# A convolution beside a gated unit on one core: a weight load placed behind the first power, and a new order of work

## The chip, the cores and the metric

The kernel runs on one core of a Trainium2 chip. The core has five engines that run their own instruction streams and meet through semaphores: TensorE (PE in the profile: matmuls, with weight loads shown as PEld), VectorE (DVE), ScalarE (ACT), GpSimd (POOL) and SyncE (SP, which here only issues DMAs). ACT and POOL issue a few DMAs too. Times are device microseconds of one execution; the time of a kernel is the median of its runs.

## The reference, cut to what matters

```python
x = A_u                                    # 2048 tokens x 512 channels, bf16
xn = layernorm(x)
# part A: a state-space convolution along the tokens, per channel d
dt = exp(log_dt)[:, None]
P = exp((dt * (A_re + 1j*A_im))[:, :, None] * arange(2048))   # 512 x 128 modes x 2048 lags
K = einsum("dn,dnl,dn->dl", Cc, P, dt * Bc).real
yA = irfft(rfft(pad(xn^T)) * rfft(pad(K)))[..., :2048]^T + xn * Dskip
# part B: a gated linear unit, 512 -> 1792 -> 512
yB = (sigmoid(xn @ w_gate) * (xn @ w_up)) @ w_down
return x + yA + yB
```

## The kernel before

**Layer norm.** The tokens are 16 groups of 128. `layernorm` (from L530) computes a group's statistics either on DVE (L542 to L544) or, for the groups in `ON_ACT`, on ACT (three activations with accumulated sums, the last at L537). GpSimd raises the variances of a stretch of groups to the power -0.5 (L495), DVE makes the bias from it (L499), and DVE (L556) or ACT normalises. The first four groups are transposed on PE (L565) and copied to `xnT`; the other twelve are stored to `x_scr` in stretches of four and come back by transposing DMAs.

**Gated unit.** Four groups of 512 tokens by 14 blocks of 128 features. Per block there are four matmuls with `wg_sb` (L1031), a sigmoid on ACT (L1040), four matmuls with `wu_sb` (L1046) and a product on DVE (L1061). The product reads the up result either from PSUM or, for the block numbers in `UEV` (14 x group + block), from `us_sb`, to which ACT has copied it (L1057). Then, for every 128 tokens, 14 matmuls with `wd_sb` (L1090), whose result is evicted to `glu_sb`.

**Convolution.** First `f_n` (L665, L667 on DVE, the squares at L656 on ACT) squares a complex number per channel and mode eleven times; GpSimd issues two DMAs per step (`f_cw`, L661) that convert the f32 result to bf16 tables `W`. Then, for four chunks of 128 channels, DVE builds two tables, G (16 entries) and H (41 entries), by complex products: `f_a` (L722, L723) multiplies, `f_b` (L727, L728) adds; some entries of H are squares made by ACT (L775) and DVE (L780, L781), and some are seeds copied from `W`. PE multiplies them in two halves (`f_k`, L806), selects (L827, L831), and the result becomes `kT`. The tokens go through small transforms: `fx` (L684, with the constant S1 and the normalised tokens), a store to `z_scr` and a load, then, for 8 pairs of units, four to each of two halves of the channels, `fm` (L874, with `m2`), `fk` (L890, with constants streamed from `c_E`), elementwise products on DVE (L895, L899), sums of them (`fsum`, L906, L907, L909), and the transform back, on PE. `SUMS` says for each pair how much is summed first: 0 means nothing and 64 matmuls (`fv`, L923), 1 means L906 and L907 and 32 matmuls (`fvs`, L935), 2 means L909 as well and 16 matmuls. The result is stored to `v_scr`, loaded again and finished by `fy` and with the last down blocks.

**The order.** The function describes 981 operations in the order of the code through `_Plan.add`: an engine, an estimated cost, a function that emits the instructions, and the operations that it depends on. `add` notes these dependencies in `users` and `left`, for a planner that isn't in the file. With `ORDER` written out, `run` goes through that list, binds the buffers and yields the operations; each engine gets its instructions in that order:

```python
        for n in ORDER or range(len(self.ops)):
            op = self.ops[n]
            for s in op.acq:
                s.idx = self.free[s.pool].pop(0)
```

The semaphores between engines come from the framework, which follows what each instruction reads and writes. `_Plan.copy` (L291 on DVE, L293 on ACT) emits a copy on DVE if its operation's number is in `ON_DVE` and on ACT otherwise.

**Loads.** `load` (L427 is the line that every DMA of this helper shows) adds a DMA on a queue. `l_wd` is the load of all down weights, 1792 KB in one DMA on SP's queue; it is operation 16. The first readers of `wd_sb` are the down matmuls of the first 128 tokens.

## Time and profile before

| | us |
|---|---|
| runs | 215.34, 214.74, 214.60 |
| median | 214.74 |
| profiled execution | 214.40 |
| its span, from the first to the last instruction | 212.7 |
| the load of the down weights, issue to landing | 15.8 |
| PE, first gate matmul | 9.18 |

The granted TensorE clock of the profiled execution is 0.998. The page cuts the span into 40 slices of 5.3 us and prints the busy share of each in tenths; these are its rows for four engines and for the DMA engines.

```profile
PE   7999998999998999999999999999999999999993
DVE  3999999998999999999999999999999999876773
ACT  3899999999999999898999999979499999632000
POOL 3324033138121000000000003700010000004000
DMA  6999939934889406798266377661997986989924
```

A row shows where an engine is full and not what it waits for: PE and DVE are at 9 nearly from end to end, DVE thins out over the last six slices, and ACT does so a little earlier. In other views a row is "start, duration, engine, line, operation, output<-inputs, sizes, count", and brackets at its end give the idle time before it and the instruction that ended it. [...]

### The profile page before, as it was taken

The page shows a single profiled execution, that of the slowest core. Times are in us where ns is not written, and L with a number is a line of the kernel's source. Part 1 is how long each engine was busy: PE and PEld are TensorE (multiplying, and loading weights), DVE is VectorE, ACT ScalarE, POOL GpSimd, SP SyncE. Part 2 cuts the span into 40 slices and gives each one's busy share as a digit, 9 for nine tenths or more (in the row PEclk, how much of TensorE's full clock was granted, in tenths as well). Part 3 has the DMA queues.
Part 4 walks back from the last instruction along what each step waited for, and adds up shares of the span by engine and source line. Part 5 has one row for each costly group of instructions (what it writes and reads, how often), then busy time and mean ns, then how long its engine had stood idle before and what let it go on. Part 6 is the DMA issues. An engine that isn't in the chain of part 4 may idle for free.

```text
span 212.7 us, 5745 instructions
## 1 busy us (share of the span) xinstructions
PE 205.2 (96%) x2251; PEld 103.2 (49%) x2251; DVE 196.2 (92%) x423; ACT 174.8 (82%) x359; POOL 33.0 (16%) x66
## 2 busy tenths in 40 slices
PE   7999998999998999999999999999999999999993
PEld 2564443444443454445466466544555646444452
DVE  3999999998999999999999999999999999876773
ACT  3899999999999999898999999979499999632000
POOL 3324033138121000000000003700010000004000
PEclk9999999999999999999999999999999999999999
DMA  6999939934889406798266377661997986989924
GB/s 188 369 420 362 278 97 232 180 54 109 175 202 228 128 5 197 215 230 253 79 182 204 99 237 207 107 101 35 277 290 201 308 252 174 296 226 244 275 102 148
DMA packets 44045, 42.36 MB, mean 199 GB/s; under 512 B 8810, under 2 KB 37747, under 8 KB 44019
## 3 DMA queue, kind: packets, MB, share of 16 engines
q1 hardware_dynamic: 39074, 36.95, 56.8%
q0 software_dynamic: 4512, 4.73, 14.1%
q8 instruction: 17, 0.28, 0.6%
q10 hardware_dynamic: 432, 0.33, 0.5%
q14 instruction: 10, 0.07, 0.1%
HBM read 25.21 MB, written 12.07 MB: 175 GB/s over the span
## 4 chain that ended last, share of the span: by engine, by line
PE 55%; DVE 30%; ACT 7%; issue 2%; POOL 2%; DMA 1%; DVEq 0%; ACTq 0%; POOLq 0%
PE bank L1090 15%; PE bank L1031 11%; PE bank L1046 10%; PE bank L890 8%; DVE hT_sb L1061 5%; ACT big L293 4%; DVE big L667 3%; DVE big L665 3%; DVE stats L542 3%; DVE big L723 2%; DVE big L722 2%; PE bank L923 2%; PE bank L806 2%; PE bank L874 2%; DVE big L604 2%
## 5 line engine op out<-in xcount | busy, mean ns | idle before, releaser
L293 ACT ACTIVATE big<-bank 128x512 bf16<-128x512 f32 (+2 forms) x147 | 77.6, 652 | 5.0 <-PE bank L806 2.9
L1031 PE MATMUL bank<-xnT,wg_sb 128*128 128x512 bf16 (+1 forms) x244 | 54.1, 362 | 1.1 <-DVE hT_sb L1061 0.7
L1046 PE MATMUL bank<-xnT,wu_sb 128*128 128x512 bf16 x224 | 52.8, 379 | 0.1
L1090 PE MATMUL bank<-wd_sb,hT_sb 128*128 128x512 bf16 (+1 forms) x238 | 50.9, 367 | 0.3 <-ACT glu_sb L293 0.2
L1040 ACT ACTIVATE hT_sb<-bank 128x512 bf16<-128x512 f32 x56 | 33.3, 648 | 3.4 <-PE bank L1031 3.4
L1090 PEld LDWEIGHTS <-hT_sb 128*128 128x128 bf16 x238 | 22.5, 98 | 25.9 <-issue 2.3
L1031 PEld LDWEIGHTS <-wg_sb 128*128 128x128 bf16 x244 | 22.7, 98 | 25.2 <-issue 4.9
L1046 PEld LDWEIGHTS <-wu_sb 128*128 128x128 bf16 x224 | 21.4, 98 | 26.3 <-issue 2.1
L722 DVE TENSOR_TENSOR big<-big 128x1024 bf16<-128x1024 bf16 (+4 forms) x40 | 27.2, 679 | 0.0
L723 DVE TENSOR_TENSOR big<-big 128x1024 bf16<-128x1024 bf16 (+4 forms) x40 | 27.0, 676 | 0.0
L895 DVE TENSOR_TENSOR big<-big 128x2048 bf16<-128x2048 bf16 x16 | 19.5, 1225 | 0.6 <-ACT big L293 0.4
L1057 ACT ACTIVATE us_sb<-bank 128x512 bf16<-128x512 f32 x29 | 19.2, 665 | 0.7 <-DVE hT_sb L1061 0.7
L890 PE MATMUL bank<-big 128*128 128x256 bf16 x160 | 19.6, 273 | 0.0
L1061 DVE TENSOR_TENSOR hT_sb<-hT_sb,bank 128x512 bf16<-128x512 bf16 x27 | 17.7, 684 | 0.4 <-ACT hT_sb L1040 0.4
L890 PEld LDWEIGHTS <-big 128*128 128x128 bf16 x160 | 15.4, 98 | 4.9 <-issue 1.0
L727 DVE TENSOR_TENSOR big<-big 128x512 bf16<-128x512 bf16 (+4 forms) x40 | 17.0, 425 | 0.0
L728 DVE TENSOR_TENSOR big<-big 128x512 bf16<-128x512 bf16 (+4 forms) x40 | 17.0, 424 | 0.0
L661 POOL DMA_DIRECT2D big<-big x24 | 13.0, 546 | 24.6 <-DVE big L667 23.4
L775 ACT ACTIVATE sq_sb<-big 128x256 bf16<-128x256 bf16 (+2 forms) x20 | 14.3, 715 | 2.0 <-DVE big L728 2.0
L293 ACT ACTIVATE big<-big 128x256 bf16<-128x256 bf16 x31 | 14.5, 480 | 0.4 <-PE bank L806 0.4
L1061 DVE TENSOR_TENSOR hT_sb<-hT_sb,us_sb 128x512 bf16<-128x512 bf16 x29 | 12.0, 424 | 0.0
L656 ACT ACTIVATE big<-big 128x1024 f32<-128x1024 f32 x11 | 11.9, 1079 | 0.0
(99 smaller groups left out, 213.5 us busy)
## 6 DMA issues: line engine op xcount, KB each, us to landing
big<-c_E SPq DMA_DIRECT2D x16, 320.0 KB, 4.7
z_scr<-big SPq DMA_DIRECT2D x16, 256.0 KB, 2.8
big<-z_scr SPq DMA_DIRECT2D x16, 256.0 KB, 4.6
v_scr<-big SPq DMA_DIRECT2D x16, 256.0 KB, 3.0
big<-big POOLq DMA_DIRECT2D x24, 128.0 KB, 3.6
big<-in_A_u_dram SPq DMA_DIRECT2D x4, 512.0 KB, 9.0
big<-v_scr SPq DMA_DIRECT2D x4, 512.0 KB, 4.4
wu_sb<-in_B_w_up_dram SPq DMA_DIRECT2D x2, 896.0 KB, 13.2
```

What stands on the lines that cost most here:

```text
L293: nc.scalar.activation(out=get(out), in_=get(in_), func=ACT.Identity)
L722: V.tensor_tensor(out=wide(outp), in0=wide(lo), in1=mre, op=ALU.mult)
L723: V.tensor_tensor(out=wide(tb()), in0=wide(lo), in1=mim, op=ALU.mult)
L727: V.tensor_tensor(out=outp[:, :, 0], in0=outp[:, :, 0], in1=tb()[:, :, 1], op=opr)
L890: T.matmul(bank(sk[kt == NKT - 1])[:, DW * c:DW * c + DW], es()[:, c, kt, :], kT[p][:, kt, :], start=kt in (0, NKT - 1), stop=kt >= NKT - 2)
L895: V.tensor_tensor(out=pp()[:, :, 0:4, :], in0=xx()[:, :, 0, :].unsqueeze(2).to_broadcast([128, 2, 4, DW]), in1=kb().unsqueeze(1).to_broadc ...
L1031: T.matmul(bank(sl)[:, c0:c1], w_at(w, CUT_G, kt, k), xnT[:, grp, kt, c0:c1], start=(kt == 0), stop=(kt == KT - 1))
L1040: S.activation(out=hT_sb[:, hs.idx, k % 2, :], in_=bank(sl), func=ACT.Sigmoid)
L1046: T.matmul(bank(sl), w_at(wu_sb, CUT_U, kt, k), xnT[:, grp, kt, :], start=(kt == 0), stop=(kt == KT - 1))
L1057: S.activation(out=us_sb[:, us.idx, :], in_=bank(sl), func=ACT.Identity)
L1061: V.tensor_tensor(out=h(), in0=h(), in1=us_sb[:, us.idx, :] if on else bank(sl), op=ALU.mult)
L1090: T.matmul(bank(po)[:, 0:c[1] - c[0]], hT_sb[:, hts[k // 2].idx, k % 2, jj * 128:(jj + 1) * 128], wd_sb[:, k, c[0]:c[1]], start=first and ...
```

## The change

The call that loads the down weights is moved from among the other loads to behind the description of the powers, and gets a dependency, `deps=[W_op[0]]`, on the first conversion. It becomes operation 87; operations 17 to 87 become 16 to 86, and the others keep their numbers. Five lists are replaced: `SUMS` (one pair of the second half of the channels goes from 2 to 1), `UEV` (29 entries become 34), `ON_DVE` (19 become 22), `ON_ACT` (token group 15 leaves it) and the whole of `ORDER`. Nothing else is changed.

```diff
 UNITS = ((0, 1, 2, 3, 4, 5, 6, 7), (0, 1, 2, 3, 4, 5, 6, 7))
-SUMS = ((0, 0, 0, 1), (1, 2, 1, 1))
+SUMS = ((0, 0, 0, 1), (1, 1, 1, 1))
...
-UEV = (5, 9, 11, 15, 16, 18, 21, 22, 24, 25, 27, 28, 29, 30, 31, 32, 33, 34, 35, 36, 37, 38, 39, 42, 43, 44, 45, 49, 54,)
+UEV = (3, 6, 8, 9, 10, 14, 15, 16, 18, 19, 20, 21, 24, 27, 28, 29, 30, 32, 33, 34, 35, 36, 37, 38, 39, 40, 41, 43, 44, 45, 46, 47, 51, 54,)
-ON_DVE = (95, 96, 97, 109, 118, 191, 193, 196, 230, 243, 375, 485, 488, 494, 507, 551, 587, 598, 600,)
+ON_DVE = (32, 95, 96, 97, 109, 118, 181, 192, 230, 289, 292, 328, 369, 489, 494, 504, 508, 517, 550, 578, 598, 601,)
-ON_ACT = (2, 8, 9, 10, 11, 13, 15,)
+ON_ACT = (2, 8, 9, 10, 11, 13,)
 ORDER = [
-    23, 0, 1, 24, 22, 29, 30, 19, 25, 2, 35, 3, 6, 10, 5, 31, 34, 43, 26, 27, 32, 36, 44, 7, 20, 37, 40, 28, 33, 21, 45,
-    38, 46, 47, 41, 39, 48, 42, 632, 626, 620, 621, 49, 633, 627, 622, 638, 634, 639, 90, 88, 89, 91, 644, 645, 655, 650,
-    4, 11, 628, 685, 92, 51, 50, 54, 656, 646, 675, 9, 55, 640, 676, 686, 93, 680, 52, 56, 53, 95, 15, 57, 58, 12, 13,
-    660, 661, 641, 665, 642, 94, 8, 635, 16, 670, 629, 647, 648, 666, 651, 681, 623, 690, 59, 60, 96, 636, 114, 637, 657,
...
+    0, 18, 23, 24, 2, 20, 1, 34, 3, 25, 26, 6, 10, 5, 22, 19, 14, 33, 28, 21, 42, 35, 29, 36, 39, 7, 40, 30, 31, 43, 37,
+    27, 41, 4, 32, 44, 45, 46, 11, 90, 91, 89, 50, 9, 15, 38, 626, 632, 47, 48, 13, 633, 620, 627, 621, 49, 12, 644, 638,
+    639, 645, 650, 655, 622, 646, 634, 665, 88, 53, 51, 651, 666, 656, 640, 685, 686, 55, 56, 628, 54, 670, 660, 671, 690,
+    623, 657, 641, 635, 92, 52, 691, 636, 101, 114, 57, 115, 58, 624, 625, 93, 629, 630, 631, 637, 87, 8, 647, 675, 672,
...
     load_x(8, 4)
     l_dk = load("SP", dskr[0:1, :], A_Dskip.rearrange("(o d) -> o d", o=1), 1 * KB)
     load_x(12, 4)
-    l_wd = load("SP", wd_sb[:], B_w_down.rearrange("(k p) d -> p k d", k=FT), 1792 * KB)
     l_m2 = load("SP", m2[:], cten["M2"].ap(), 256 * KB, pkt=2048)
     l_sw = load("SP", sw[:], cten["SW"].ap(), 96 * KB, pkt=768)
 
...
             cur_op = pl.add("DVE", 1.2, f_n, [s_op] + W_op[-2:-1], PLAD + k * 0.01)
         W_op.append(c_op)
 
+    l_wd = load("SP", wd_sb[:], B_w_down.rearrange("(k p) d -> p k d", k=FT), 1792 * KB, deps=[W_op[0]])
     layernorm(4, 8, PLN1)
     layernorm(8, 12, PLN2)
     layernorm(12, 16, PLN3)
```

## The prediction

> **What bounds the kernel now.** First the head of the page, then busy time in four stretches that I cut at the places where VectorE (DVE) hands work to TensorE (PE).

> ```profile
> span 212.7 us, 5745 instructions
> PE 205.2 (96%) x2251; PEld 103.2 (49%) x2251; DVE 196.2 (92%) x423; ACT 174.8 (82%) x359; POOL 33.0 (16%) x66
> ```
> ```profile
> core 0: us, PE busy (x) PEld busy (x) DVE busy (x) ACT busy (x) POOL busy (x), PEclk, DMA share, GB/s
> 3.58:76.69 73.11, 70.82 (x382) 32.37 (x381) 71.09 (x167) 70.08 (x138) 20.76 (x32) 1.00 0.79 213
> 76.69:150.97 74.28, 73.81 (x1160) 39.26 (x1160) 74.13 (x169) 68.94 (x151) 6.82 (x16) 1.00 0.60 162
> 150.97:184.92 33.95, 33.91 (x530) 18.97 (x528) 33.05 (x54) 31.25 (x64) 0.86 (x1) 1.00 0.87 256
> 184.92:212.70 27.78, 24.45 (x178) 11.75 (x176) 17.89 (x38) 3.28 (x7) 2.51 (x3) 0.99 0.72 201
> ```

> PE's 96% alone would say that PE is the bound. The stretches say more: from 3.58 to 150.97 DVE idles 2.02 + 0.15 us of 147.39, PE 2.29 + 0.47. Two engines are full at once, and DVE's results pace PE's convolution work. These are the first and last hand-overs, in the order of time on both engines, and PE's end.

> ```profile
> 76.25 0.44 DVE L728 TENSOR_TENSOR big<-big 128x512 bf16<-128x512 bf16 x1
> 76.49 1.67 PE L806 MATMUL bank<-big 128*32 128x82 bf16 x128 [0.18 <-ACT big L293]
> ...
> 183.90 0.55 DVE L906 TENSOR_TENSOR big<-big 128x768 bf16<-128x768 bf16 x1
> 184.37 0.55 DVE L907 TENSOR_TENSOR big<-big 128x768 bf16<-128x768 bf16 x1
> 185.13 0.86 PE L935 MATMUL bank<-big 32*64 32x512 bf16 x32
> ...
> 206.17 3.23 PE L1090 MATMUL bank<-wd_sb,hT_sb 128*128 128x256 bf16 x28
> ```

> L728 is the last step of chunk 0's table G; L806 (`f_k`) multiplies it and starts 0.24 after L728 does, having waited 0.18. At the end, L935 starts 0.2 after the last half-sum L907. From 76.49 on PE is full: the last matmul ends at 206.17 + 3.23 = 209.40, 132.91 us after `f_k` began. The profiled execution took 214.4, so 5.0 us lie behind that end. So the time is: when can `f_k` of chunk 0 start, plus PE's work from there.

> **The dependency that the change names.** `deps` fills a list that only the planner reads; with an order written out, the kernel emits in that order, and an engine waits only where two instructions touch the same tile. `wd_sb` shares no tile with the powers. I cost the named wait at nothing: it is not in the program. What is real is the place on SP's queue.

> ```profile
> 13.81 0.46 SPq L427 DMA_DIRECT2D wd_sb<-in_B_w_down_dram  x1
> ...
> wd_sb<-in_B_w_down_dram SPq DMA_DIRECT2D x1, 1792.0 KB, 15.8
> ...
> 34.15 0.40 PE L684 MATMUL bank<-big 32*64 32x512 bf16 x2
> ...
> 35.51 1.69 PE L1090 MATMUL bank<-wd_sb,hT_sb 128*128 128x512 bf16 x7
> ```

> The load is the fourteenth issue of SP in both orders. It lands at 13.81 + 15.8 = 29.6, 5.9 us ahead of its first reader (35.51). Moved past it are the load of S1 (32 KB, now behind it, first read at 34.15) and that of `dskr` (1 KB, now ahead); the load of tokens 8 to 11 goes ahead of the second half of the up weights. S1 keeps some 20 us from its issue to its reader, and the bytes in flight are the same. Cost nothing; the cover is the 5.9 us for the weights.

> **The order, DVE ahead of `f_k`.** I counted, engine by engine, what stands ahead of chunk 0's `f_k` in the two orders. DVE's queue ahead of it grows. Spacings, start to start, of the rows:

> ```profile
> 27.01 1.28 DVE L1061 TENSOR_TENSOR hT_sb<-hT_sb,bank 128x512 bf16<-128x512 bf16 x2
> 28.20 0.69 DVE L542 BATCH_NORM_STATS2 stats<-big 128x6 f32<-128x512 bf16 x1
> ...
> 29.21 1.27 DVE L1061 TENSOR_TENSOR hT_sb<-hT_sb,bank 128x512 bf16<-128x512 bf16 x2
> ...
> 35.37 0.27 DVE L291 COPY big<-big 128x256 bf16<-128x256 bf16 x1
> 35.50 0.68 DVE L1061 TENSOR_TENSOR hT_sb<-hT_sb,bank 128x512 bf16<-128x512 bf16 x1
> ...
> 76.60 0.42 DVE L1061 TENSOR_TENSOR hT_sb<-hT_sb,us_sb 128x512 bf16<-128x512 bf16 x1
> 76.93 1.22 DVE L722 TENSOR_TENSOR big<-big 128x2048 bf16<-128x2048 bf16 x1
> 78.07 1.22 DVE L723 TENSOR_TENSOR big<-big 128x2048 bf16<-128x2048 bf16 x1
> ```

> - Operation 237, two 128x2048 products of chunk 1, moves from just behind chunk 0's `f_b` to ahead of it: 2 x (78.07 - 76.93) = +2.28.
> - Token group 15's statistics go from ACT to DVE: 29.21 - 28.20 = +1.01.
> - The copy of the second transposed token tile goes to DVE (bf16, PSUM, 128x512). No row shows it there: above the 0.13 of a 128x256 copy from SBUF (35.50 - 35.37), below the 0.60 of a product that reads PSUM ((28.20 - 27.01)/2). I take 0.45, nearer the row with PSUM. Chunk 0's first G copy also goes to DVE, +0.13; two seed copies leave or fall behind, -0.27.
> - Products of the GLU (L1061): one that reads SBUF takes 76.93 - 76.60 = 0.33, from PSUM 0.60. Numbers 16 and 22 move ahead (+0.66), 19, 24 and 25 behind (-1.26). Of those ahead, seven go from PSUM to SBUF and four the other way: -3 x 0.26 = -0.79.

> Sum: 2.28 + 1.01 + 0.45 + 0.13 - 0.27 + 0.66 - 1.26 - 0.79 = **+2.21 us** on DVE. What comes off is a wait:

> ```profile
> 44.23 1.05 POOL L661 DMA_DIRECT2D big<-big  x2 [3.20 <-DVE big L667]
> 46.98 3.21 POOL L495 TENSOR_TENSOR ln_ri<-ln_ve,half 128x4 f32<-128x4 f32 x1 [1.70 <-ACT ln_ve L537]
> ...
> 50.22 0.16 DVE L499 SCALAR_TENSOR_TENSOR ln_nb<-mv,ln_ri 128x4 f32<-128x4 f32 x1 [0.92 <-POOL ln_ri L495]
> ```

> DVE stood 0.92 for the power -0.5 of tokens 8 to 11, which GpSimd began late because ACT's statistics were late. In the new order ACT makes these statistics at least 5 us sooner, ahead of copies that now follow. GpSimd then begins right behind its conversions, which follow a squaring step that stands about 1.5 us sooner: 44.23 + 1.05 - 1.5 = 43.8, ending near 47.0, while DVE, with more ahead of it, comes to L499 near 51.0. The 0.92 goes whole. `f_k` thus starts at 76.49 + 2.21 - 0.92 = **77.78**.

> **PE, ahead of `f_k` and behind it.**

> ```profile
> 11.08 8.46 PE L1031 MATMUL bank<-xnT,wg_sb 128*128 128x256 bf16 x52 [0.43 <-ACT xnT L293]
> ...
> 35.05 0.41 PE L684 MATMUL bank<-big 32*64 32x512 bf16 x6 [0.50 <-ACT us_sb L1057]
> ...
> 67.47 1.02 PE L1031 MATMUL bank<-xnT,wg_sb 128*128 128x512 bf16 x4 [0.71 <-DVE hT_sb L1061]
> ...
> 88.73 0.59 PE L1090 MATMUL bank<-wd_sb,hT_sb 128*128 128x512 bf16 x2 [0.18 <-ACT glu_sb L293]
> ...
> 123.39 0.95 PE L923 MATMUL bank<-big 32*64 32x512 bf16 x29 [0.21 <-DVE big L899]
> ```
> ```profile
> 164.12 0.97 PE bank L1031 x4
> ...
> 173.68 0.86 PE bank L1031 x4
> 174.54 0.57 PE bank L935 x16
> ...
> 179.99 0.79 PE bank L935 x32
> ```

> The second fence is from the chain of waits: start, time, matmuls. Ahead of `f_k` PE now has one up block more (0.86) and starts about 0.17 later by a hand count of the first loads. If none of its waits of 0.18, 0.43, 0.50 and 0.71 went, it would reach `f_k` at 76.49 + 0.86 + 0.17 = 77.5; if all went, at 75.7. DVE's 77.78 is later either way, so it sets the start.

> From `f_k` on: 132.91 - 0.86 (that up block) + 0.22 (`SUMS`: one pair's product sums are left to PE, 32 matmuls at 0.79 for 16 at 0.57) + 0.22 (two more changes of matmul layout, 0.97 - 0.86 = 0.11 each) - 0.39 (the waits of 0.18 and 0.21, which DVE's and ACT's earlier work removes) = 132.10. PE ends at 77.78 + 132.10 = 209.88, the execution at 214.88: 0.48 above its own 214.4. The runs' median is 214.74, so **215.2**.

> That later hand-overs don't become late is the weak step. DVE's whole work changes by +1.01 (statistics) + about 1.05 (fourteen copies in, eleven out, 0.35 each) - 1.30 (five more products read SBUF) - 0.94 (two sums fewer, 184.37 - 183.90 each): -0.2. DVE is no more loaded; the moved 2.28 is missing behind `f_k`.

> [...] GpSimd's power took 3.21 at 46.98, and there is a row of 1.39 for the same form:

> ```profile
> 14.83 1.39 POOL L495 TENSOR_TENSOR ln_ri<-ln_ve,half 128x4 f32<-128x4 f32 x1 [7.25 <-DVE ln_ve L544]
> ```

> [...]

> **The rivals.**
> - **A, as summed** (0.41): 215.2, between 214.6 and 215.8.
> - **B, faster** (0.25): the new order also closes DVE's small gaps ahead of `f_k` (2.02 - 0.92 = 1.10) and the unknown copy costs its lower bound (0.32 less). `f_k` starts at 77.78 - 1.42 = 76.36, still behind PE's 75.7; PE ends at 208.46, the run at 213.5, median 213.8. For it: PE has little else that could hold it. Against: those gaps are many and small, and nothing in the order names them.
> - **C, slower** (0.31): DVE waits again for the power on GpSimd. It decides if GpSimd ends after about 51.0, 4 us later than I count; that needs ACT's statistics late again, or a power over 7.2 us long. Then the 0.92 stays: 216.1. The same price comes from any one DVE wait of that length ahead of `f_k`, since PE has no slack behind it.
> - **D, the wait is real** (0.03): the load is issued after the first conversion.

> ```profile
> 17.48 1.32 POOL L661 DMA_DIRECT2D big<-big  x2 [1.25 <-DVE ln_nb L499]
> ...
> big<-big POOLq DMA_DIRECT2D x24, 128.0 KB, 3.6
> ```

> It would be issued at 17.48 + 1.32 + 3.6 = 22.4 and land at 38.2, 2.7 after its reader's 35.51. At least 0.3 of this is hidden by PE's wait for `f_k`: 215.2 + 2.4 = 217.6.

> **How the numbers follow.** Likeliest is A: 215.2. The range 213.5 to 217.0 holds A, B and C with their unknown copy (0.13 to 0.60) and leaves out D and the far ends. About 0.3% (0.64 us) is what a measurement of this kernel tells from no change. B falls below it: faster 0.25. C and D lie above: 0.34, to which A's upper edge adds 0.02. A's rest, 0.39, is within.

> **What would show it.** The trace after should have: the weights' load issued near 14, as before, without a wait for GpSimd; operation 237's two 1.22 us products ahead of chunk 0's last L728; no wait at L499 for the power; `f_k` near 77.8 and released by DVE; then PE unbroken for 132.1. A start of `f_k` before 76.9 speaks for B, a DVE wait of about 0.9 ahead of it for C. The forecast is wrong in kind if PE stands for DVE behind chunk 1, where I took all hand-overs to fit.

## The result, and the profile after

| | before | after |
|---|---|---|
| runs, us | 215.34, 214.74, 214.60, 214.22 | 216.35, 217.05, 218.37, 217.13 |
| median, us | 214.67 | 217.09 |
| profiled execution, us | 214.40 | 216.35 |
| its span, us | 212.7 | 214.4 |

The ratio of the times is 1.0117, with a 95% interval of 1.0084 to 1.015: the kernel became slower by about 1.2%, 2.4 us. The forecast was 215.2, so it had the sign of its middle value right and a size of one fifth, and the time lies 0.09 above its range. The profiled executions differ by 1.95.

The page's first lines, and the same four stretches as before (the last one ends with the span, at 214.40). The columns of the second fence are stretch, length, busy time of PE, PEld, DVE, ACT and POOL with counts, granted clock, DMA share and GB/s.

```profile
span 214.4 us, 5762 instructions
PE 203.7 (95%) x2241; PEld 103.1 (48%) x2267; DVE 196.4 (92%) x427; ACT 174.4 (81%) x356; POOL 41.3 (19%) x66
```
```profile
3.58:76.69 73.11, 70.21 (x374) 32.74 (x380) 71.98 (x168) 70.09 (x137) 29.95 (x38) 1.00 0.81 221
76.69:150.97 74.28, 73.49 (x1153) 38.80 (x1162) 73.97 (x173) 68.29 (x150) 5.97 (x11) 1.00 0.58 156
150.97:184.92 33.95, 31.86 (x539) 18.32 (x545) 31.88 (x56) 28.99 (x60) 1.72 (x2) 1.00 0.88 249
184.92:214.40 29.48, 25.94 (x176) 12.46 (x176) 18.58 (x34) 5.71 (x11) 1.60 (x2) 1.00 0.69 193
```

The third stretch is the one to see. PE was busy 33.91 of its 33.95 us before and 31.86 after: 2.05 us are missing there. (PE's count on the page is 2241 and not 2267; a few of its records are missing in this trace, so weight loads are the better place to look.) The two hand-overs that frame it, in the order of time on PE:

```profile
77.84 1.34 PE L806 MATMUL bank<-big 128*32 128x82 bf16 x120
...
150.78 1.67 PE L806 MATMUL bank<-big 128*32 128x82 bf16 x128
152.38 3.20 PE L1090 MATMUL bank<-wd_sb,hT_sb 128*128 128x512 bf16 x13
155.51 0.86 PE L827 MATMUL bank<-big,sw 128*32 128x96 bf16 x64
156.20 0.22 PE L831 MATMUL bank<-dskr,ident 128*32 128x64 bf16 x2
158.15 0.82 PE L1031 MATMUL bank<-xnT,wg_sb 128*128 128x512 bf16 x3 [1.73 <-issue]
```

And the same place before:

```profile
150.78 1.67 PE L806 MATMUL bank<-big 128*32 128x82 bf16 x128
152.38 3.20 PE L1090 MATMUL bank<-wd_sb,hT_sb 128*128 128x512 bf16 x14
155.41 1.03 PE L1031 MATMUL bank<-xnT,wg_sb 128*128 128x512 bf16 x4
156.37 0.63 PE L874 MATMUL bank<-big,m 64*32 64x512 bf16 x16
156.93 0.86 PE L827 MATMUL bank<-big,sw 128*32 128x96 bf16 x64
```

`f_k` of chunk 0 starts at 77.84, 0.06 from the forecast and 1.35 later than before. That delay is gone by chunk 3, whose `f_k` starts at 150.78 in both kernels. Behind it, after the selection (L827, which the new order puts ahead of the gate block and of L874), PE stands 1.73 us in front of a gate block. The bracket says "issue": it waited for nothing that the profile shows. From that `f_k` to the start of the last down matmuls (206.17 before, 207.84 after) the distance grew from 55.39 to 57.06, by 1.67. The stand is about as long as that difference; how much of it comes back when the stand goes is a question for e2.

### The profile page after: what moved, and what is told of

It reads as the page before. It is cut to its first block, busy times and chain, and to the rows that moved or that the text cites. A ratio compares the mean times of both kernels' runs of the same rounds, so it can differ in the third digit from the quotient of the medians.

```text
span 214.4 us, 5762 instructions
## 1 busy us (share of the span) xinstructions
PE 203.7 (95%) x2241; PEld 103.1 (48%) x2267; DVE 196.4 (92%) x427; ACT 174.4 (81%) x356; POOL 41.3 (19%) x66
## 4 chain that ended last, share of the span: by engine, by line
DVE 60%; PE 25%; ACT 8%; issue 4%; DMA 2%; POOL 0%; SPq 0%; DVEq 0%; ACTq 0%
DVE big L722 10%; DVE big L723 10%; PE bank L1090 7%; DVE big L728 6%; DVE hT_sb L1061 6%; DVE big L727 5%; PE bank L1031 5%; PE bank L1046 4%; PE bank L890 4%; ACT big L293 4%; DVE big L895 3%; DVE big L666 3%; DVE big L603 3%; DVE big L664 3%; DVE stats L541 2%
## 5 line engine op out<-in xcount | busy, mean ns | idle before, releaser
L293 ACT ACTIVATE big<-bank 128x512 bf16<-128x512 f32 (+2 forms) x146 | 79.9, 670 | 5.3 <-PE bank L806 2.8
L1031 PE MATMUL bank<-xnT,wg_sb 128*128 128x512 bf16 (+1 forms) x233 | 52.5, 361 | 3.0 <-issue 1.9
L1090 PE MATMUL bank<-wd_sb,hT_sb 128*128 128x512 bf16 (+1 forms) x231 | 49.9, 367 | 1.5 <-DVE hT_sb L1061 1.0
L1031 PEld LDWEIGHTS <-wg_sb 128*128 128x128 bf16 x244 | 22.8, 98 | 26.2 <-issue 5.3
L1090 PEld LDWEIGHTS <-hT_sb 128*128 128x128 bf16 x238 | 22.5, 98 | 26.4 <-issue 3.2
L722 DVE TENSOR_TENSOR big<-big 128x1024 bf16<-128x1024 bf16 (+4 forms) x40 | 26.4, 661 | 0.2
L723 DVE TENSOR_TENSOR big<-big 128x1024 bf16<-128x1024 bf16 (+4 forms) x40 | 26.3, 657 | 0.0
L1057 ACT ACTIVATE us_sb<-bank 128x512 bf16<-128x512 f32 x34 | 22.4, 701 | 0.7 <-DVE hT_sb L1061 0.7
L660 POOL DMA_DIRECT2D big<-big x24 | 13.0, 546 | 38.5 <-DVE big L666 29.6
L890 PE MATMUL bank<-big 128*128 128x256 bf16 x160 | 19.6, 273 | 0.1
L775 ACT ACTIVATE sq_sb<-big 128x256 bf16<-128x256 bf16 (+2 forms) x20 | 15.0, 748 | 3.6 <-DVE big L728 2.6
L890 PEld LDWEIGHTS <-big 128*128 128x128 bf16 x160 | 15.4, 98 | 4.5 <-DMA big<-z_scr 0.4
L293 ACT ACTIVATE big<-big 128x256 bf16<-128x256 bf16 x30 | 16.3, 579 | 0.1
L727 DVE TENSOR_TENSOR big<-big 128x512 bf16<-128x512 bf16 (+4 forms) x40 | 16.3, 407 | 0.1
L728 DVE TENSOR_TENSOR big<-big 128x512 bf16<-128x512 bf16 (+4 forms) x40 | 16.2, 406 | 0.0
L1061 DVE TENSOR_TENSOR hT_sb<-hT_sb,bank 128x512 bf16<-128x512 bf16 x22 | 14.4, 677 | 1.8 <-PE bank L1046 1.8
L1061 DVE TENSOR_TENSOR hT_sb<-hT_sb,us_sb 128x512 bf16<-128x512 bf16 x34 | 13.9, 412 | 0.1
## 6 DMA issues: line engine op xcount, KB each, us to landing
big<-big POOLq DMA_DIRECT2D x24, 128.0 KB, 3.0
```

Of the source, the lines that this page charges most:

```text
L293: nc.scalar.activation(out=get(out), in_=get(in_), func=ACT.Identity)
L722: V.tensor_tensor(out=wide(outp), in0=wide(lo), in1=mre, op=ALU.mult)
L723: V.tensor_tensor(out=wide(tb()), in0=wide(lo), in1=mim, op=ALU.mult)
L727: V.tensor_tensor(out=outp[:, :, 0], in0=outp[:, :, 0], in1=tb()[:, :, 1], op=opr)
L728: V.tensor_tensor(out=outp[:, :, 1], in0=outp[:, :, 1], in1=tb()[:, :, 0], op=opi)
L890: T.matmul(bank(sk[kt == NKT - 1])[:, DW * c:DW * c + DW], es()[:, c, kt, :], kT[p][:, kt, :], start=kt in (0, NKT - 1), stop=kt >= NKT - 2)
```

## The experiments

**Where exactly PE stands.** The weight loads have all their records. This is the timeline of PEld in after:

```profile
155.51 0.72 PEld L827 LDWEIGHTS <-sw 128*32 128x32 bf16 x64 [0.43 <-DVE big L291]
156.16 0.14 PEld L831 LDWEIGHTS <-ident 128*32 128x32 bf16 x2
156.35 0.10 PEld L1031 LDWEIGHTS <-wg_sb 128*128 128x128 bf16 x1
158.14 0.33 PEld L1031 LDWEIGHTS <-wg_sb 128*128 128x128 bf16 x3 [1.70 <-issue]
```

The block's first weight load runs at 156.35 and its second at 158.14. The four matmuls of the block read the same tiles and write the same bank, so a buffer or a DMA that the block needed would have held the first. The page has a queue that could be late and that no semaphore tells of:

```profile
q8 instruction: 18, 0.29, 0.6%
```

These are 18 packets of 16,384 bytes (packets, bytes in MB, share of the DMA engines). The trace has the time of each. I counted PE's own instructions (a matmul and its weight load are two, a wait or a drain of its sequencer is one: 2 x 2267 + 22 = 4556 in after) and set the packets against them. The stand lies at instruction 3523. Borders every 256 instructions from there, forwards and back, have one packet each: 18 borders and 18 packets in after, 17 and 17 in before (a border is the place where PE passes from one 256 to the next). The theory (I, below): PE had come to the end of its instructions. The rival (II): a transfer or a buffer was late in a way that the profile doesn't name.

**e1: after, once more.** No edit.

> The changed kernel once more, nothing edited. Theory I (PE runs out of instructions: in the trace of after it stands 1.70 us at 158.14 inside a gate block, between the first and the second of four equal matmuls, and the row of the instruction queue that brings 16 KB landed at 156.76): the stand is there again, within 1 us of the same place and between 1 and 3 us long, and the median is 216 to 218. Theory II (PE waits there for a buffer or a z_scr load that happened to be late in that one execution): the stand is gone or at another instruction in this execution.

Measured: median 217.68 (216.35 to 219.54), ratio to before 1.015 [1.009, 1.021]. This is the PE list of the view of waits (engine, line, releaser; total, times, longest):

```profile
PE bank L1031 <- issue: 2.6, 2, 2.4
```

The stand is there again, at the same instruction 3523, 2.4 us long, ending at 159.97 and not within 1 us of 158.14: the whole execution was 1.15 later by `f_k` of chunk 3. The page's row of the granted clock in 40 slices shows why, and why this execution took 219.54:

```profile
PEclk9999999799999999999999999999979999999999
```

In that row a 9 stands for full speed. The trace's clock records give half the clock for 3.4 us from 37.6 and again from 160.5, each just behind a stand of PE (1.0 for DVE, and this one of 2.4). Not each execution has such windows: the traced one of after stood 0.99 near 36 us and 1.70 here, at a clock of 1.00. The spread of after goes with it: of the 8 executions of after and e1, the three with a clock below 1 (0.992, 0.992 and 0.984) took 217.90, 218.37 and 219.54, the others 216.35 to 217.47.

**e2: the same program, its instructions shifted.** The tiny matmuls are the only edit; they lie where PE waits for the first tokens (the first gate matmul is at 9.42 here, 9.44 in after, by the first record of its operation).

```diff
             for _ in range(n):
                 T.matmul(bank(wsl), glu_sb[:, 0, 0:128], glu_sb[:, 0, :], start=True, stop=True)
+            if n > 6:
+                for j in range(104):
+                    t = 32 * (j % 4)
+                    T.matmul(bank(wsl)[t:t + 32, 0:8], glu_sb[:, 0, 0:32], glu_sb[:, 0, 0:8], start=True, stop=True, tile_position=(0, t))
```

> After, with 104 tiny matmuls (208 instructions, 32 columns of weights by 8) behind the nine warm-up matmuls at the very start, where PE waits for the first tokens; no other instruction is changed. Counted from the traces, PE's instructions come in pieces of 256, and PE passes from one to the next at instruction 3523; the shift puts that border 208 instructions earlier, into f_k of chunk 3, and the next one 48 later, into fk of the second half. Theory I: the stand of 1.70 at 158 falls below 0.5, the time falls by 1.0 to 1.9 against after, less up to 0.6 for the start: 214.8 to 216. Theory II: the stand stays, the time is that of after plus 0 to 0.6.

Measured: median 215.48 of ten executions (214.87 to 218.60; 215.23 without the slowest), ratio to before 1.0051 [1.0029, 1.0072], and no stand near 158 in the one that was traced. The third stretch shows it:

```profile
150.97:184.92 33.95, 33.45 (x546) 18.99 (x552) 33.46 (x59) 29.96 (x62) 1.73 (x2) 1.00 0.93 264
```

PE has 33.45 of 33.95 again. Adding 208 useless instructions made the kernel faster by 1.6 us against after's first runs (217.09) and by 2.2 against those of the same chip (217.68). Theory II has nothing to explain that with: no transfer, buffer or wait was edited. In the traced execution the last down matmuls start at 206.90, 0.94 sooner than in after and not 1.70: PE now waits 0.49 at 196.82 for a load of `v_scr`, which it doesn't in after. Two of the ten executions still have a clock of 0.992 (216.23 and 218.60).

**e3: before, shifted,** by the same edit with 80 matmuls.

```diff
+                for j in range(80):
```

> Before, with 80 of the same tiny matmuls (160 instructions) at the start, nothing else changed. The shift makes a whole piece of 256 instructions coincide with f_k of chunk 3, which PE runs in 1.6 us; in the traces the next piece came 0.1 to 4 us after PE had passed a border, took 1 us, and was used 1.4 us later. Theory I: PE stands 1 to 5 us right behind f_k of chunk 3 (near 152.4) for no releaser, and the kernel is slower by 0.5 to 5 us. Theory II: no such stand, slower by no more than 0.6.

A miss for theory I as I had it: median 215.03, ratio 1.0030 [1.0011, 1.0049], and no stand of PE behind `f_k`. The trace says why. Here the packet started at 150.42, 0.97 before PE passed the border, and landed at 151.50; I had assumed that a packet starts at a border or behind it. It may start ahead of one. So what counts is the time between the packet's landing and PE's arrival at the end of its 256, and not the number of small matmuls alone. The shift did cost 0.64 us. Its trace has two things, among others, that the trace of before doesn't: a stand of 0.29 at the next border (158.89, 1.54 after that packet's landing) and a wait of 0.59 for a copy of DVE at 188.06. A shift is not harmless by itself.

**e4: the selection put back behind the gate block.**

The selection is operation 374; the evictions 883 and 874 on ACT move ahead of it too. This is the one line of `ORDER` that differs, cut:

```diff
-    872, 374, 883, 874, 375, 376, 899, 900, 493, 503, 506, ...
+    872, 883, 899, 493, 874, 374, 375, 376, 900, 503, 506, ...
```

> After, with the selection of chunk 3 (f_sel, 132 instructions in 0.8 us) put behind one gate block and the fm of units 0 and 1, the order that before has there; ACT's two evictions 883 and 874 are listed earlier to free the banks, in the same order on ACT. Theory I: PE gets 1.4 us of work with 40 instructions ahead of the 132, so it reaches instruction 3523 about 0.9 us later: the stand falls from 1.7 to 0.5 to 1.0, the time by 0.5 to 1.2. Theory II (a late z_scr load or buffer): the gate block or fm stands just as long.

```profile
157.02 0.69 PE L827 MATMUL bank<-big,sw 128*32 128x96 bf16 x47
158.00 0.39 PE L827 MATMUL bank<-big,sw 128*32 128x96 bf16 x17 [0.28 <-issue]
158.18 0.22 PE L831 MATMUL bank<-dskr,ident 128*32 128x64 bf16 x2
159.35 1.25 PE L890 MATMUL bank<-big 128*128 128x256 bf16 x10 [0.95 <-ACT big L293]
```

The stand moved with instruction 3523 into the selection and shrank to 0.28, more than expected. The time followed in part: 216.88, ratio 1.0107 [1.0082, 1.0132], which is 0.80 below e1 on the same chip, as expected, and 0.21 below after's first runs. Most of what the stand gave up came back as 0.95 of waiting for ACT's copies of the selection's result, which L890 reads. In the new order the early selection had a use.

**e5: four loads later,** in `ORDER` of after.

```diff
-    472, 548, 459, 520, 519, 377, 547, 481,
+    472, 459, 520, 519, 481,
...
-    495, 576, 507,
+    495, 507,
...
-    510, 533, 521,
+    510, 533, 548, 377, 547, 576, 521,
```

> After, with four loads of SP (z_scr of units 4 and 5, one of units 6 and 7, and the constant S2) listed behind the first c_E load of the second half, so that they are issued near 161 and not between 149.9 and 155.2; no instruction count changes. Theory I with the cause of the late piece in the DMA traffic: the piece of instructions that started at 155.73, 3.97 after PE had passed the border, starts before 154, the stand of 1.70 falls below 0.5, and the kernel is faster than after by 0.8 to 1.9. Theory I with a fixed delay: piece and stand as before. Theory II: the stand is no longer than in after, for PE waited for one of these loads, but the piece still starts near 155.7.

Measured: 218.01, ratio 1.0187 [1.0136, 1.0238]. The packet started at 155.61 (155.73 in after), the stand stayed at 1.5, and PE waited 2.0 more at L874 for one of the moved loads. That speaks against theory II, whose loads were no longer there, but not for a delay of its own: from 152 to 156 the DMA engines were as full as before (share 0.94 against 1.01), since the other loads filled the place.

**e6: operation 237 back behind `f_b` of chunk 0,** in e2's kernel.

```diff
-    722, 237, 86,
+    722, 86,
...
-    761, 220, 766,
+    761, 220, 237, 766,
```

> The kernel e2_after_shift208 with operation 237 (two 128x2048 products of chunk 1) put back behind f_b of chunk 0. Theory A (DVE's whole work up to chunk 3 paces the middle, and what stands ahead of f_k of chunk 0 only moves that one start): f_k of chunk 0 starts 1.0 to 2.2 sooner than its 77.91, f_k of chunk 3 stays within 0.3 of 150.87, and the time within 0.4 of the 215.48 of e2. Theory B (the forecast's sum: the start of f_k of chunk 0 sets the end): f_k of chunk 3 and the end come sooner by 0.7 to 1.3.

Neither theory: 217.48, ratio 1.0137 [1.0112, 1.0162]. Timelines of DVE and PE:

```profile
76.54 0.43 DVE L1065 TENSOR_TENSOR hT_sb<-hT_sb,us_sb 128x512 bf16<-128x512 bf16 x1 [1.35 <-ACT us_sb L1061]
```
```profile
77.89 1.11 PE L810 MATMUL bank<-big 128*32 128x82 bf16 x96
80.57 0.49 PE L810 MATMUL bank<-big 128*32 128x82 bf16 x32 [1.57 <-DVE hT_sb L1065]
```

(The lines are four higher than in after: L1065 is the product, L810 is `f_k`.) `f_k` started at 77.89 with or without 237 ahead of it (77.91 in e2). Without it DVE waited 0.60 at 72.52 for squares made by ACT and 1.35 for an eviction on ACT, and the last quarter of `f_k` waited 1.57 for a product that now stood behind 237. In this order the 2.28 us of 237 were not on the path to `f_k`; most of them filled waits for ACT.

**e7: the load's place in the queue alone,** in `ORDER` of before: S1 (8) behind the down weights (16).

```diff
-    94, 8, 635, 16, 670,
+    94, 635, 16, 8, 670,
```

> Before, with the load of S1 issued behind that of the down weights, the one thing that the moved load does to the queue; all else as before. Theory: nothing waits, S1 lands ahead of 34.15, and the time is that of before within 0.3. Rival: fx of the first tokens waits for S1 near 34, and the time grows by what it waits.

Measured: 214.34, ratio 1.0001 [0.999, 1.0012]. Nothing, as expected. Its traced execution, the slowest of ten (214.91), shows something else: a stand of PE among equal weight loads in before's own order, at another border.

```profile
143.52 0.11 PEld L1090 LDWEIGHTS <-hT_sb 128*128 128x128 bf16 x2 [0.30 <-issue]
144.40 1.62 PEld L1090 LDWEIGHTS <-hT_sb 128*128 128x128 bf16 x9 [0.77 <-issue]
```

The packet of that border landed at 143.00, 1.41 before PE went on.

**e8: token group 15's statistics back on ACT,** in e2's kernel.

```diff
-ON_ACT = (2, 8, 9, 10, 11, 13,)
+ON_ACT = (2, 8, 9, 10, 11, 13, 15,)
```

> The kernel e2_after_shift208 with token group 15's statistics back on ACT. Theory A (DVE paces up to chunk 3): DVE has 1.01 less to do there, f_k of chunk 3 comes 0.4 to 1.0 sooner than 150.87, the time falls by as much, and PE's stand of 1.0 for DVE at 36.7 falls by as much. Rival B (ACT is full there too, 35.31 and 33.49 us of 37.00 busy on DVE and ACT from 3 to 40): the products come late for lack of sigmoids, f_k of chunk 0 later by 0.5 to 1.5 and the time within 0.4 of e2 or above.

Rival B: 216.28, ratio 1.0087 [1.006, 1.0113]. PE's wait for DVE at 36.7 fell from 1.0 to 0.3, but it waited 0.84 at 31.37 and 0.79 at 36.74 for sigmoids of ACT; `f_k` of chunk 0 came at 78.88, 0.97 later. DVE, ACT and PE are full together there, and 1 us moved from one to the other is paid on that other.

**e9 and e10: `SUMS` alone,** taken back in e2's kernel (e9) and made in before (e10).

```diff
 # e9
-SUMS = ((0, 0, 0, 1), (1, 1, 1, 1))
+SUMS = ((0, 0, 0, 1), (1, 2, 1, 1))
 # e10
-SUMS = ((0, 0, 0, 1), (1, 2, 1, 1))
+SUMS = ((0, 0, 0, 1), (1, 1, 1, 1))
```

> The kernel e2_after_shift208 with SUMS as before (the second pair of the second half sums once more on DVE: 16 matmuls of 0.57 on PE instead of 32 of 0.79). Theory A (PE sets the time from chunk 3 on): faster than e2 by 0.1 to 0.3, so 215.2 to 215.4, and its last half-sum reaches PE no later than e2's 185.44. Rival B (DVE's extra 0.94 comes late): the same as e2 or slower by up to 0.9, with a wait of PE for fsum.

> Before with SUMS as after, the one part alone. Theory A: 0.22 more on PE and nothing else: 0.05% to 0.2% slower than before. Rival B (DVE's 0.94 less lets PE go on sooner at the following pairs): not slower, or faster by up to 0.2%.

e9: 215.59, ratio 1.0079 [1.0055, 1.0103], not faster than e2: rival B without the wait that I had named. Its third set of matmuls on half-sums (L935 in before, L939 here) starts at 180.34 and not 179.81, the fourth at 185.98 and not 185.44, and it made this up at the end, where e2 waited 0.5 for a `v_scr` load and e9 did not; the last down matmuls start at 206.87 in e9 and 206.90 in e2. e10: 215.08, ratio 1.0042 [1.0027, 1.0057]. In before's order the change of `SUMS` costs more than its 0.22: from `f_k` of chunk 3 to the last down matmuls the trace has 0.41 more; the medians differ by 0.8. Where the other 0.4 lie, one profile can't say.

**e11: six loads later,** as e5 and with the loads of units 2 and 3.

```diff
-    472, 548, 459, 520, 519, 377, 547, 481,
+    472, 459, 481,
...
-    510, 533, 521,
+    510, 533, 520, 519, 548, 377, 547, 576, 521,
```

> After, with six loads (the five of z_scr and of S2 issued between 149.9 and 155.2 and one more issued at 155.2, those of units 2 and 3 among them) listed behind the first c_E load of the second half. In e5 four of them went, the DMA engines' share from 152 to 156 fell only from 1.01 to 0.94, and the piece still came at 155.61. Here the share in 152 to 156 must fall below 0.6, or the test says nothing. Theory I with DMA traffic as the cause of the late piece: it starts before 154.0 and the stand at 158 is below 0.5. Theory I with a delay of its own: it starts near 155.6 and the stand is 1.3 to 2.4 as before. The time isn't the question: PE then waits longer for the loads of units 2 and 3.

The packet started 1.74 after the border (3.97 in after), and PE passed instruction 3523 at 157.75 without the stand. The share from 152 to 156 was 0.86, so by the condition that I had set the test says nothing; it was 0.49 from 149 to 152 (0.92 in after), with the whole execution 1.4 later here. I take it as a sign that the traffic delays the packet, and leave it open. The time (221.1) holds a wait of 3.6 at L874 for the moved loads.

**e12: a shift of 24,** the edit of e2 with 12 matmuls.

```diff
+                for j in range(12):
```

> After, with 12 of the tiny matmuls (24 instructions) at the start. Theory I: the border moves 24 instructions back, from the gate block into the selection of chunk 3 (f_sel, 132 instructions ahead of that block), so PE stands 1.5 to 2.5 us between two of its matmuls near 156.1, and the gate block behind it runs without one; the time is that of after, 216.4 to 217.9. Theory II (the gate block waits for something of its own): the stand stays between its first and second matmul.

```profile
157.95 0.63 PEld L831 LDWEIGHTS <-sw 128*32 128x32 bf16 x55 [0.42 <-DVE big L910]
159.34 0.15 PEld L831 LDWEIGHTS <-sw 128*32 128x32 bf16 x9 [0.76 <-issue]
159.40 0.14 PEld L835 LDWEIGHTS <-ident 128*32 128x32 bf16 x2
159.59 0.55 PEld L1035 LDWEIGHTS <-wg_sb 128*128 128x128 bf16 x4
```

The border lies 9 weight loads from the end of the selection (L831 here), and there PE stands; the gate block (L1035) runs through. With 0.76 it is half of what I expected, and a second stand of 0.8 appeared one piece earlier, in the down matmuls (at 143.45). This execution reached `f_k` of chunk 3 at 153.48, 2.7 later than after; like e1 it had run at half the clock for 3.4 us from 37.6. Median 217.07, ratio 1.0116 [1.0094, 1.0138]: the time of after.

**The pieces in all traces**, from the packets of q8 and the count of PE's instructions:

```
         border 3267   packet           PE goes on    landing    stand
         passed                         past 3523     to going on
before   151.78        155.05-156.02    157.41        1.39       none
after    151.76        155.73-156.76    158.14        1.38       1.70
e1       152.90        157.49-158.55    159.97        1.42       2.4
e4       151.77        155.67-156.64    157.99        1.35       0.28
e5       151.78        155.61-156.71    158.23        1.52       1.5
e11      153.15        154.89-155.98    157.75        1.77       none
e12      154.11        157.02-157.96    159.34        1.38       0.76
```

Wherever PE stands at this border it goes on 1.35 to 1.52 after the packet has landed. Before reached the border 1.39 after the landing: it was just in time. After is worse by both ends: its packet is 0.7 later, and PE, with the selection's 132 instructions moved ahead of 40 that take 1.5 us, would have been at the border at 156.45, 0.96 earlier. 0.7 + 0.96 = 1.7.

The rule can be put to every border of the 14 traces, before and after among them: I set the landing of each packet against the time at which PE passes the border that ends its 256 instructions. Of the 236 borders PE passed none sooner than 1.35 after the landing. And where it passed one between 1.35 and 1.55 after, there are more stands named "issue", at other borders and in other matmuls: 0.77 in e7 (144.40), 1.08 on the weight loads in e12 (143.45), 0.32 in e6 (160.63), 0.29 in e3 (158.89). So a late packet held PE where PE came to the border early, in before's order too. What makes the packet late stays open.

## Why the forecast was wrong, step by step

- **The dependency isn't in the program; the place in the queue costs nothing.** Right: in after SP issued the load from 9.33 to 13.66, ahead of the first conversion at 16.7, and e7 gives 1.0001.
- **The wait for GpSimd goes.** Right to half a microsecond. I had counted 43.8 and 47.0 for the power and 51.0 for DVE:

```profile
43.53 2.94 POOL L494 TENSOR_TENSOR ln_ri<-ln_ve,half 128x4 f32<-128x4 f32 x1
```
```profile
50.74 0.15 DVE L498 SCALAR_TENSOR_TENSOR ln_nb<-mv,ln_ri 128x4 f32<-128x4 f32 x1
```

  There is no bracket on either row. Rival C did not happen: the power took 2.94, less than the 3.21 of before, and nobody waited for it. A power over 7.2 us long, which rival C names beside late statistics, is shown by no run: the six powers of this form in before and after took 1.02 to 3.21. What sets their length isn't shown either: DVE was busy all 1.39 us of the power at 14.83 in before and 2.32 of the 3.21 of that at 46.98, and in after it was busy all through one of 1.02 (at 32.69) as through that of 2.94.
- **`f_k` starts at 77.78, set by DVE.** The time was right (77.84), the reason was not, and the 0.06 is luck. The row of L806 has no wait: PE came there by its own work, while DVE's last L728 started at 77.27, which with the 0.24 of before would have let `f_k` start at 77.51. On its way PE had waited 0.65 and 0.99 near 36 us, where before has one wait of 0.50. I had bounded PE's arrival at 77.5 by its old waits and added no new ones, and rival B's 76.36 I had held against PE's lower bound of 75.7 alone. e6 shows that the largest term of DVE's sum, 2.28, was for the most part covered by waits for ACT.
- **The middle fits.** I had called it the weak step. It held: the up block (-0.86) and the two waits (-0.39) take 1.25 of the 1.35 off again, and chunk 3 is reached at 150.78 in both. The other 0.10 doesn't come from the changes of matmul layout: by the shapes of PE's weight loads there are 29 between the two `f_k` in both kernels. From there to the last down matmuls there are 31 for 30, one more where I had counted two.
- **From `f_k` on, PE's work and its waits: 132.10.** This is the step that failed: the forecast put PE's wait for its own instructions at nothing. It took the gaps between PE's instructions to be either work or waits for another engine, and took PE's supply of instructions as free. The profiled execution took 207.84 - 77.84 = 130.00 to the start of the last matmuls and 3.23 for them, 133.23 in all, 1.13 too much; with 0.06 from `f_k` and 0.28 behind PE's end (5.28 for 5.0) that is the 1.47 by which the profiled execution missed its 214.88. The stand of 1.70 lies in it; taken off on paper it leaves 131.53, but e2, which runs without it, has 132.22. e4 and e12 show that the stand goes where the border goes, and e2 that it goes away with it. The half-clock windows follow stands in some executions (e1, e12); e2 still has a clock of 0.992 in two of ten, so they aren't shown to go with the stand.
- **`SUMS` at 0.22.** Mis-sized: alone in before's order it costs 0.4 (trace) to 0.8 (medians), in after's order undoing it gains nothing (e9).
- **What is left without the stand.** e2 is 0.5% above before, 1.1 us; the forecast was 0.48 us above. PE's way from `f_k` of chunk 0 to its end, 132.22 in e2, is 0.12 from the forecast, but by other parts: 1.33 less than before up to `f_k` of chunk 3, where the terms -0.86 and -0.39 were, and 0.64 more behind it, of which 0.49 is the wait for `v_scr` that no term held. The order alone thus costs 0.6 to 1.5 us by e2's interval, somewhat more than forecast, and after costs 1.6 to 2.2 on top by the medians. That the stand and the windows are all of it isn't shown.

No version among these beats before.

## What to carry to other kernels

Where a program is unrolled and one engine runs hundreds of very short instructions in a row (here 388 in 2.5 us of PE's time), read its waits named "issue", and look for a stand between two instructions that need the same things. Reordering such blocks moves the engine's demand for instructions (here PE came to the border 0.96 us sooner), which no dependency shows. A shift by some tiny instructions at the start moves the borders and leaves the order alone: if the stand moves with the border, this is its cause. Whether a shift is also a cure depends on where the border comes to lie: 208 instructions took about 2 us off, 24 took nothing, and 160 in before cost 0.6. A move that adds work ahead of a hand-over is not a cost until one knows that the engine didn't wait there for someone else.
